# Attention P·V in 64-row tiles, maxima transposed on VectorE, and a new slot table for the scores, in a fused attention and GEGLU kernel

## Chip, cores and metric

One core of a Trainium2 chip runs the whole program. The metric is the device time of one execution in microseconds (us). The kernel before was run three times: 1045.97, 1046.92 and 1047.18 us, median 1046.92 us.

## What is computed

The input x is 2048 tokens by 640 features. The result is x plus a sliding-window attention of LN(x) plus a gated feed-forward of LN(x):

```python
q, k, v = split(xn @ wqkv)            # 32 heads of 20
scores = einsum("bhqd,bhkd->bhqk", q, k) * 20 ** -0.5
mask = (i - j >= 0) & (i - j < 256)   # each query sees itself and 255 keys before it
o = softmax(where(mask, scores, -1e9)) @ v
A = o @ wo
h = gelu(xn @ w_gate) * (xn @ w_up)   # 640 -> 1728
return x + A + h @ w_down
```

## The kernel before

The kernel keeps everything transposed, with features on partitions and tokens in the free dimension. The program has three stages: layer norm and the first projections (to about 118 us), the attention loop with projections mixed into it (about 118 to 560 us), and the rest of the feed-forward with the output projections (560 us to the end). The change touches the second stage; its spread-out sums of the input prepare the third.

**The loop.** `attention()` walks 32 units. A unit is four heads (group g) by 512 queries (chunk c = u % 4). Each unit is 14 slots long (`NS`). A slot first runs deferred work that has come due (`tick`), then may run a burst of row-maximum work (`BURSTS` = slots 0, 4 and 8), then P·V of the unit before (slot 0 only, followed by a second burst), then the score pieces that the table `SCORES` names for this slot, then pending VectorE work (`flush`), then a few instructions from a list of idle GpSimd work (`release`), then loads, and at last `pull_fill`, which issues dense projection matmuls (lines L110: `ps_d`, `ps_v`) until the slot has its share of TensorE work. The order in each engine's queue is the order of the code; no scheduler changes it for TensorE, VectorE and ScalarE.

**Row maxima.** `max_pair` computes scores for a 128-query block of two heads with the bf16 keys, in matmuls of 60 rows by 32 columns (L523): eight small tiles of the array, in two PSUM banks, 288 columns in each tile. VectorE masks and reduces each bank (L527). A burst is two such pairs, so four banks. A unit needs eight pairs, computed one or two units ahead. When all are in, VectorE negates them and splits them into two bf16 parts (L536, L537; `nm`), and six slots after that burst `max_end` transposes `nm` by a TensorE matmul against an identity (L544, `ps_n`), ScalarE copies the result out of PSUM (L546), and a DMA on ScalarE's queue writes it as two rows into the query stack `qs` (L547), where the score matmul takes it in as two more rows of its contraction.

**Scores.** `exp_piece` (L582) computes a bank of scores of one head, keys on partitions, 512 columns; ScalarE takes the exponential into `P` (L584). There are twelve pieces to a unit: three arrangements X, Z and Y of the key blocks by four heads. When the fourth head of an arrangement is in, GpSimd clears the masked triangles (L595, L598). Before, `SCORES` visits five slots: 0, 2, 4, 8 and 10, with 1, 4, 2, 2 and 3 pieces.

**P·V.** `av_unit` (L600 to L620) multiplies P by V for a unit in one PSUM bank: four heads side by side as 128x32 tiles of the array, six key blocks each (four where c = 0), in float32, which TensorE does in two passes. ScalarE evicts the bank to `ob` (L613), and three slots later SP stores four head blocks and the row sums (L617, L618).

**Banks.** Every PSUM tile named here (`ps_m`, `ps_e`, `ps_o`, `ps_n`) comes from one ring of six banks, handed out in order of use; a matmul that takes a bank waits until the one that read it last (VectorE for `ps_m`, ScalarE for the others) is done. The dense matmuls have banks of their own.

**Input sums.** `x_sums` makes sums of the input on GpSimd (L740) for the third stage: eight groups of ten small operations, 50 slots apart, two slots between operations in a group.

In the diff's order, the places are: `SCORES` near the top, the memory of `nm` (`nms`), the end of `max_pair` and `max_end`, `av_unit`, and the spacing in `attention()`.

Of the kernel before, what the change touches and what calls it, by code (L numbers as in the profile page):

```python
# [9 lines left out]
F32 = mybir.dt.float32  # L10
# [60 lines left out]
def block_kernel(ctx, tc, x, wqk, wv, wgu, wdo, wdl, out):  # L71
# [269 lines left out]
    nms = [st1.tile([128, 4, 2, 4, 4], BF, name=f"nm{i}") for i in range(2)]  # L341
    for nm in nms:
        nc.gpsimd.memset(nm, 0.0)

    def first_chunk(xs, wr0, wr5, lp):
        halves = slice(0, 256), slice(256, 512)

# [150 lines left out]
    def bank(name):  # L498
        return psr.tile([128, C], F32, name=name, tag="ring")
# [3 lines left out]
    def max_pair(u, i):  # L503
# [37 lines left out]
    def max_end(u):  # L541
        nm = maxes.pop(u)
        ps = bank("ps_n")
        nc.tensor.matmul(ps[:, 0:128], nm.rearrange("p z a j b -> p (z a j b)"), identb, start=True, stop=True)  # L544
        mr = ap.tile([32, 128], BF, name="mr", tag="mr")
        nc.scalar.activation(mr, ps[0:32, 0:128], AF.Copy)  # L546
        late(lambda: nc.scalar.dma_start(qs[u % NQ][SR:SR + 2].rearrange("p j t -> p (j t)"), mr))  # L547

    def pieces(c):
        b = 4 * c  # L550
# [37 lines left out]
    def clear(u, bi):  # L588
        c = u % NC
        pt = pts[u, bi]  # L590
        for p in pieces(c)[bi]:
            for col, diag in diag_tail(*p, c):
# [4 lines left out]
                else:  # L597
                    nc.gpsimd.affine_select(out=a, in_=a, pattern=[[0, 4], [-1, 128]], compare_op=OP.is_ge,  # L598
                                            fill=0.0, base=-1, channel_multiplier=1)

    def av_unit(u):
        g, c = divmod(u, NC)
        o, v = bank("ps_o"), vtiles[g]
        todo = [(pts[u, bi], *p) for bi, ps in enumerate(pieces(c)) for p in ps]
        for i, (pt, kb, col, q0, n) in enumerate(todo):
            assert (id(v), kb) in done, (u, kb)
            for j in range(4):
                w0_ = kb * 84 + 21 * j
                nc.tensor.matmul(o[32 * j:32 * j + 32, q0:q0 + n], v[:, w0_:w0_ + 32], pt[:, j, col:col + n],  # L609
                                 start=i == 0, stop=i == len(todo) - 1, skip_group_check=True,  # L610
                                 tile_position=(0, 32 * j))
        ob = ap.tile([128, C], F32, name="ob", tag="ob", bufs=1)
        nc.scalar.activation(ob, o, AF.Copy)  # L613

        def store():
            for j in range(4):
                nc.sync.dma_start(od[c].rearrange("(d h) t -> h d t", h=H)[4 * g + j], ob[32 * j:32 * j + DH, :])  # L617
            nc.sync.dma_start(sd[c][4 * g:4 * g + 4, :], ob[DH::32, :])  # L618

        defer(3, store)  # L620

    def load_gu(f):
        raws = []
# [181 lines left out]
    def attention():  # L805
# [703 lines left out]
```

## Time and profile before

| what | value |
|---|---|
| median of three runs | 1046.92 us |
| the profiled execution | 1046.71 us |
| its span on the core | 1045.0 us |
| granted TensorE clock | 0.999 of full speed |
| attention stage, 118 to 560 us | 442 us |

The profiled execution is 1.7 us longer than its span; that lies around the span. PE is TensorE (PEld its weight loads), DVE is VectorE, ACT is ScalarE, POOL is GpSimd, and SP the engine that issues most DMAs. In a timeline row stand the start, the duration, the engine, the line, the operation, its tiles with shapes and how many instructions the row gathers. A row's end may lie past the start of the next, because matmuls are pipelined; the step from one start to the next is therefore the time that a piece of TensorE's work takes.

### The profile page before, as it was taken

To read this page: it belongs to the slowest core of one execution; us is meant where nothing else is said; L and a number is where in the kernel's file an instruction comes from. 1 tells how busy PE (TensorE), PEld (TensorE's weight loads), DVE (VectorE), ACT (ScalarE), POOL (GpSimd) and SP (SyncE) were. 2 spreads that over 40 slices of the span, in tenths; PEclk is the share of its full clock that TensorE was granted. 3 is DMA by queue.
4 is the path that set the end of the run, shared out by engine and by line. 5 is a ranking of instruction groups with operands and counts; after the bars stand their busy time and mean duration, and the time that the engine had idled before them with its cause. 6 is when DMAs were issued, how large, how long until landed. Compare 5 with 4: busy or idle time off the path is not lost.

```text
span 1045.0 us, 25814 instructions
## 1 busy us (share of the span) xinstructions
PE 1034.0 (99%) x9533; PEld 826.2 (79%) x9533; DVE 717.1 (69%) x2007; ACT 513.6 (49%) x1088; POOL 335.9 (32%) x511
## 2 busy tenths in 40 slices
PE   8999999999999999999999999999999999999998
PEld 8987666666677766666667888888888999999998
DVE  8745656666655556666663678877656888888887
ACT  4444666765665666555656522223324553333332
POOL 5222767766464458464634111110110000000000
PEclk9999999999999999999999999999999999999999
DMA  5552465545332355444322556677217864443342
GB/s 200 189 150 61 136 185 157 174 152 183 98 117 74 106 148 153 129 131 140 103 80 82 191 193 235 220 254 246 100 61 255 272 232 137 136 128 114 124 136 92
DMA packets 105192, 158.76 MB, mean 152 GB/s; under 512 B 15421, under 2 KB 60093, under 8 KB 105065
## 3 DMA queue, kind: packets, MB, share of 16 engines
q1 hardware_dynamic: 102680, 150.95, 45.1%
q10 hardware_dynamic: 2384, 6.16, 1.8%
q8 instruction: 75, 1.23, 0.5%
q14 instruction: 53, 0.43, 0.1%
HBM read 101.78 MB, written 54.92 MB: 150 GB/s over the span
## 4 chain that ended last, share of the span: by engine, by line
PE 89%; DVE 3%; DMA 3%; POOL 2%; SPq 1%; ACT 1%; issue 1%; DVEq 0%; POOLq 0%
PE ps_g L953 21%; PE ps L1220 21%; PE ps_d L110 19%; PE ps_e L582 7%; PE ps_v L110 7%; PE ps_o L609 7%; PE ps_m L523 4%; PE ps_g L110 1%; DMA qs<-qd 1%; SPq L494 1%; PE ps_t L181 1%; DMA qd<-pt 1%; POOL pt L259 1%; PE ps_d L356 1%; POOL wql L643 0%
## 5 line engine op out<-in xcount | busy, mean ns | idle before, releaser
L527 DVE CUSTOM_DVE_ANT_0 junk<-ps_m,mask 128x288 bf16<-128x288 f32 (+2 forms) x512 | 227.9, 445 | 155.0 <-PE ps_m L523 97.2
L584 ACT ACTIVATE P<-ps_e 128x512 f32<-128x512 f32 (+2 forms) x384 | 195.6, 578 | 59.8 <-PE ps_e L582 56.1
L1220 PE MATMUL ps<-wb,at 128*128 128x320 f32 x999 | 155.9, 309 | 0.0
L1220 PEld LDWEIGHTS ps<-wb,at 128*128 128x128 f32 x999 | 148.9, 188 | 0.2
L595 POOL TENSOR_SCALAR_AFFINE_SELECT P<-P 128x512 f32<-128x512 f32 x128 | 84.6, 663 | 139.1 <-ACT P L584 138.1
L582 PE MATMUL ps_e<-qs,ks 124*128 124x128 bf16 (+2 forms) x704 | 107.4, 277 | 0.6 <-DVE mx L527 0.5
L110 PE MATMUL ps_d<-xh,wqh 128*128 128x512 f32 x350 | 104.3, 410 | 0.0
L110 PE MATMUL ps_d<-xl,wqh 128*128 128x512 f32 x350 | 104.3, 409 | 0.0
L110 PE MATMUL ps_d<-xh,wql 128*128 128x512 f32 x350 | 103.9, 409 | 0.0
L1220 PE MATMUL ps<-wt,at 128*128 128x320 f32 x552 | 89.3, 309 | 0.4 <-DVE u L1058 0.4
L582 PEld LDWEIGHTS <-ks 124*128 124x128 bf16 x704 | 50.9, 98 | 46.5 <-issue 29.0
L609 PE MATMUL ps_o<-P,v 128*32 128x384 f32 (+2 forms) x1408 | 84.9, 386 | 0.7 <-POOL P L598 0.7
L1220 PEld LDWEIGHTS ps<-wt,at 128*128 128x128 f32 x552 | 82.9, 188 | 0.9 <-DVE u L1058 0.9
L598 POOL TENSOR_SCALAR_AFFINE_SELECT P<-P 128x512 f32<-128x512 f32 x112 | 70.3, 638 | 33.6 <-ACT P L584 33.6
L1174 ACT ACTIVATE at<-ss 128x512 fp32r<-128x512 f32 x59 | 37.3, 632 | 87.6 <-DVE ss L1058 87.5
L103 POOL TENSOR_TENSOR wql<-wr,wqh 128x640 fp32r<-128x640 f32 x11 | 17.6, 1607 | 174.8 <-PE ps_g L953 149.5
L609 PEld LDWEIGHTS ps_o<-P,v 128*32 128x32 f32 x1408 | 41.0, 109 | 40.5 <-issue 20.4
L110 PEld LDWEIGHTS ps_d<-xh,wql 128*128 128x128 f32 x350 | 63.9, 189 | 11.1 <-issue 0.4
L110 PEld LDWEIGHTS ps_d<-xl,wqh 128*128 128x128 f32 x350 | 63.8, 189 | 10.4 <-issue 0.2
L110 PEld LDWEIGHTS ps_d<-xh,wqh 128*128 128x128 f32 x350 | 63.5, 189 | 10.7 <-issue 0.2
L259 POOL TENSOR_TENSOR pt<-r,pt 128x512 bf16<-128x512 f32 x40 | 46.8, 1169 | 63.2 <-ACT pt L258 63.0
L613 ACT ACTIVATE ob<-ps_o 128x512 f32<-128x512 f32 x32 | 19.1, 598 | 86.3 <-PE ps_o L609 76.1
(194 smaller groups left out, 1846.8 us busy)
## 6 DMA issues: line engine op xcount, KB each, us to landing
hr<-hd SPq DMA_DIRECT2D x104, 128.0 KB
hd<-he SPq DMA_DIRECT2D x50, 256.0 KB
wr<-wgu SPq DMA_DIRECT2D x27, 320.0 KB
qs<-qd SPq DMA_DIRECT2D x64, 120.0 KB
ks<-kd SPq DMA_DIRECT2D x64, 120.0 KB
xi<-x SPq DMA_DIRECT2D x16, 320.0 KB
qs<-qd SPq DMA_DIRECT2D x64, 80.0 KB
ks<-kd SPq DMA_DIRECT2D x64, 80.0 KB
```

The lines of the kernel that those rows point to most:

```text
L110: nc.tensor.matmul(ps, a(k), b(k), start=n == 0, stop=n == 3 * nk - 1)
L259: nc.gpsimd.tensor_tensor(out=pt[:, l, :], in0=r, in1=pt[:, 1, :], op=OP.subtract)
L523: nc.tensor.matmul(ps[32 * h:32 * h + 32, lo:hi], q[rows, j, q0:q0 + 32], keys, start=True, stop=True, tile_position=(64 * r, 32 * h))
L527: nc.vector.tensor_tensor_reduce(out=junk[:, 0:n], in0=ps[:, 0:n], in1=mask[:, 288 - n:288], scale=1.0, scalar=NEG, op0=OP.add, op1=OP.max ...
L582: nc.tensor.matmul(ps[:, col:col + n], k[0:QROWS, j, kc:kc + 128], q[0:QROWS, j, q0:q0 + n], start=True, stop=True)
L584: nc.scalar.activation(pt[:, j, lo:hi], ps[:, lo:hi], AF.Exp, scale=SCALE)
L595: nc.gpsimd.affine_select(out=a, in_=a, pattern=[[0, 4], [1, 128]], compare_op=OP.is_ge, fill=0.0, base=0, channel_multiplier=-1)
L598: nc.gpsimd.affine_select(out=a, in_=a, pattern=[[0, 4], [-1, 128]], compare_op=OP.is_ge, fill=0.0, base=-1, channel_multiplier=1)
L609: nc.tensor.matmul(o[32 * j:32 * j + 32, q0:q0 + n], v[:, w0_:w0_ + 32], pt[:, j, col:col + n], start=i == 0, stop=i == len(todo) - 1, ski ...
L953: nc.tensor.matmul(ps, i, j, start=first and n == 0, stop=n == len(work) - 1, skip_group_check=True)
L1174: nc.scalar.activation(hi[:, 3:7], s, AF.Copy)
L1220: nc.tensor.matmul(ps[bank][:, 0:HD], *work[bank][j], start=bank not in begun, stop=final[p, bank] == n and j == len(work[bank]) - 1, skip ...
```

## The change

- P·V (`av_unit`): a key block of 128 rows is cut into two halves of 64 rows, so that eight 64x32 tiles of the array are in use and not four 128x32 ones. The upper and lower halves add up in two PSUM banks (`halves`). Each half takes only the columns that its 64 keys can be seen from (at most 320), and pairs of half blocks are issued together (`windows`). ScalarE evicts both banks, the second into a part of the P tile that is free by then, and GpSimd adds the two (a new operation, one slot later). The store comes four slots later, not three.
- Maxima: VectorE negates into `nm` and transposes it in 32x32 blocks (`nc.vector.transpose`) into `mr`; `max_end` is then four DMAs on SP. TensorE's transpose, ScalarE's copy and the DMA on ScalarE's queue are gone.
- `SCORES`: the visit in slot 0 is gone; slots 2, 4, 8 and 10 have 4, 2, 3 and 3 pieces.
- Input sums: five slots between operations, not two.

```diff
-SCORES = {0: range(0, 1), 2: range(1, 5), 4: range(5, 7), 8: range(7, 9), 10: range(9, 12)}
+SCORES = {2: range(0, 4), 4: range(4, 6), 8: range(6, 9), 10: range(9, 12)}
...
-            nm = nms[u % 2]
-            maxes[u] = nm
+            nm = ap.tile([128, 2, 4, 4], BF, name="nm", tag="nm")
+            mr = maxes[u] = ap.tile([128, 32], BF, name="mr", tag="mr")
...
-                nc.vector.tensor_scalar(nm[:, 0, 0], mx, -1.0, None, op0=OP.mult)
-                nc.vector.scalar_tensor_tensor(nm[:, 0, 1], mx, -1.0, nm[:, 0, 0], op0=OP.mult, op1=OP.subtract)
+                nc.vector.tensor_scalar(nm[:, 0], mx, -1.0, None, op0=OP.mult)
+                nc.vector.scalar_tensor_tensor(nm[:, 1], mx, -1.0, nm[:, 0], op0=OP.mult, op1=OP.subtract)
+                nc.vector.transpose(mr, nm.rearrange("p z j b -> p (z j b)"))
...
     def max_end(u):
-        nm = maxes.pop(u)
-        ps = bank("ps_n")
-        nc.tensor.matmul(ps[:, 0:128], nm.rearrange("p z a j b -> p (z a j b)"), identb, start=True, stop=True)
-        mr = ap.tile([32, 128], BF, name="mr", tag="mr")
-        nc.scalar.activation(mr, ps[0:32, 0:128], AF.Copy)
-        late(lambda: nc.scalar.dma_start(qs[u % NQ][SR:SR + 2].rearrange("p j t -> p (j t)"), mr))
+        mr = maxes.pop(u)
+        for h in range(4):
+            dst = qs[u % NQ][SR:SR + 2].rearrange("p j (b h r) -> p j b h r", h=4, r=32)[:, :, :, h]
+            nc.sync.dma_start(dst, mr[32 * h:32 * h + 32])
...
+    def windows(c):
+        r = {}
+        for bi, ps in enumerate(pieces(c)):
+            for kb, col, q0, n in ps:
+                for h in range(2):
+                    first = 128 * (kb - 4 * c) + 64 * h
+                    lo = max(0, first) if kb else 0
+                    hi = min(C, first + 320)
+                    r[h, kb - 4 * c] = bi, kb, col + lo - q0, lo, hi - lo
+        pairs = [(0, 0), (-2, -2), (2, -1), (-1, 2), (1, 1), (3, 3)] if c else [(d, d) for d in range(4)]
+        return [[(h, *r[h, d]) for h, d in enumerate(p)] for p in pairs]
...
-        o, v = bank("ps_o"), vtiles[g]
-        todo = [(pts[u, bi], *p) for bi, ps in enumerate(pieces(c)) for p in ps]
+        halves, v = [bank("ps_o") for _ in range(2)], vtiles[g]
+        todo = windows(c)
...
-                nc.tensor.matmul(o[32 * j:32 * j + 32, q0:q0 + n], v[:, w0_:w0_ + 32], pt[:, j, col:col + n],
-                                 start=i == 0, stop=i == len(todo) - 1, skip_group_check=True,
-                                 tile_position=(0, 32 * j))
-        ob = ap.tile([128, C], F32, name="ob", tag="ob", bufs=1)
-        nc.scalar.activation(ob, o, AF.Copy)
+                for h, bi, kb, col, q0, n in pair:
+                    rows, w0_ = slice(64 * h, 64 * h + 64), kb * 84 + 21 * j
+                    nc.tensor.matmul(halves[h][32 * j:32 * j + 32, q0:q0 + n], v[rows, w0_:w0_ + 32],
+                                     pts[u, bi][rows, j, col:col + n], start=i == 0, stop=i == len(todo) - 1,
+                                     skip_group_check=True, tile_position=(64 * h, 32 * j))
+        ob, other = ap.tile([128, C], F32, name="ob", tag="ob", bufs=1), pts[u, 2][:, 0, :]
+        nc.scalar.activation(ob, halves[0], AF.Copy)
+        nc.scalar.activation(other, halves[1], AF.Copy)
+        defer(1, lambda: nc.gpsimd.tensor_tensor(out=ob, in0=ob, in1=other, op=OP.add))
...
-        defer(3, store)
+        defer(4, store)
...
-                at(XS0 + XSN * i + 2 * j, when_free, fn)
+                at(XS0 + XSN * i + 5 * j, when_free, fn)
```

How this moves the rows of a queue is shown at three places. The first is TensorE's queue in slot 0 of a unit, at the end of P·V and the start of the second burst of maxima; `ps_o` is P·V's bank, `ps_m` a maxima bank. Before:

```order
L609 MATMUL ps_o_2430<-P_2329,v_479 32x384 [waits Pool_49]
L609 MATMUL ps_o_2430<-P_2329,v_479 32x384 x2
L609 MATMUL ps_o_2430<-P_2329,v_479 32x384 [waits Activation_49]
L609 MATMUL ps_o_2430<-P_2329,v_479 32x128 [waits Pool_49]
L609 MATMUL ps_o_2430<-P_2329,v_479 32x128 x3
L523 LDWEIGHTS qs1_167
L523 MATMUL ps_m_2457<-ks0_169,qs1_167 32x288 [waits PE_49]
```

And after, where `ps_o_2473` and `ps_o_2474` are the two halves:

```order
L617 MATMUL ps_o_2474<-P_2372,v_475 32x320
L617 MATMUL ps_o_2473<-P_2372,v_475 32x128 [waits Pool_49]
L617 MATMUL ps_o_2474<-P_2372,v_475 32x64
L617 MATMUL ps_o_2473<-P_2372,v_475 32x128
L617 MATMUL ps_o_2474<-P_2372,v_475 32x64
L519 LDWEIGHTS qs1_167
L519 MATMUL ps_m_2526<-ks0_169,qs1_167 32x288 [waits DVE_49]
L519 LDWEIGHTS qs1_167
L519 MATMUL ps_m_2527<-ks0_169,qs1_167 32x288 [waits DVE_49]
```

The halves alternate with unequal widths in the last pair, and the first matmul of the burst behind them, which waited for TensorE's own earlier work, now waits for VectorE.

The second place is TensorE's queue in slot 8, behind the burst of that slot (`ps_e` is a bank of scores, `ps_d` a dense bank). Before:

```order
L523 MATMUL ps_m_2625<-ks1_170,qs2_168 32x288
L582 LDWEIGHTS ks2_171
L582 MATMUL ps_e_2637<-qs0_166,ks2_171 128x256 [waits DVE_49]
L582 LDWEIGHTS ks3_172
L582 MATMUL ps_e_2637<-qs0_166,ks3_172 128x256
L582 LDWEIGHTS ks3_172
L582 MATMUL ps_e_2642<-qs0_166,ks3_172 128x128 [waits Activation_49]
L582 LDWEIGHTS ks3_172
L582 MATMUL ps_e_2642<-qs0_166,ks3_172 128x384
L110 MATMUL ps_d_2538<-xl0_80,wqh_2066 128x512 x4
```

And after:

```order
L577 MATMUL ps_e_2705<-qs0_166,ks2_171 128x256 [waits Activation_49]
L577 LDWEIGHTS ks3_172
L577 MATMUL ps_e_2705<-qs0_166,ks3_172 128x256
L577 LDWEIGHTS ks2_171
L577 MATMUL ps_e_2709<-qs0_166,ks2_171 128x256 [waits DVE_49]
L577 LDWEIGHTS ks3_172
L577 MATMUL ps_e_2709<-qs0_166,ks3_172 128x256
L577 LDWEIGHTS ks3_172
L577 MATMUL ps_e_2714<-qs0_166,ks3_172 128x128 [waits DVE_49]
L577 LDWEIGHTS ks3_172
L577 MATMUL ps_e_2714<-qs0_166,ks3_172 128x384
L110 MATMUL ps_d_2599<-xl0_80,wqh_2086 128x512 x4
```

Three pieces stand there in place of two, and the third takes a bank that VectorE has to free: that of the first tile of the very burst ahead of it.

The third place is SP's queue near slot 6 of a unit, where `max_end` now puts its rows (`od`, `sd` are P·V's stores, `kd` a store of keys, `ks` a load of keys):

```order
L628 DMA sd1_97<-ob_2188 4x512 [waits DMAHW5_49]
L268 DMA kd2_90<-pt_2084 32x3x512 [waits DMAHW6_49,Pool_49]
L268 DMA kd2_90<-pt_2084 80x3x512 [waits DMAHW7_49]
L268 DMA kd2_90<-pt_2084 16x3x512 [waits DMAHW0_49]
L542 DMA qs0_166<-mr_2219 2x16x32 [waits DMAHW1_49,DVE_49]
L542 DMA qs0_166<-mr_2219 2x16x32 [waits DMAHW2_49]
L542 DMA qs0_166<-mr_2219 2x16x32 [waits DMAHW3_49]
L542 DMA qs0_166<-mr_2219 2x16x32 [waits DMAHW4_49]
L490 DMA ks1_170<-kd1_89 40x1024 [waits DMAHW5_49,PE_49]
```

The four L542 rows are new; before, nothing stood there between the stores and the next load, and TensorE's queue had one row `ps_n` in that slot.

More of the change, by code (lines that the diff above doesn't have):

```diff
@@ L340, in block_kernel @@
     ks = [st1.tile([128, 4, C], BF, name=f"ks{i}") for i in range(NK)]
-    nms = [st1.tile([128, 4, 2, 4, 4], BF, name=f"nm{i}") for i in range(2)]
-    for nm in nms:
-        nc.gpsimd.memset(nm, 0.0)
     def first_chunk(xs, wr0, wr5, lp):
@@ L599, in clear @@
                                             fill=0.0, base=-1, channel_multiplier=1)
+    def windows(c):
[9 more added lines that the diff above has]
+        return [[(h, *r[h, d]) for h, d in enumerate(p)] for p in pairs]
     def av_unit(u):
         g, c = divmod(u, NC)
-        o, v = bank("ps_o"), vtiles[g]
-        todo = [(pts[u, bi], *p) for bi, ps in enumerate(pieces(c)) for p in ps]
-        for i, (pt, kb, col, q0, n) in enumerate(todo):
-            assert (id(v), kb) in done, (u, kb)
+        halves, v = [bank("ps_o") for _ in range(2)], vtiles[g]
+        todo = windows(c)
+        for i, pair in enumerate(todo):
             for j in range(4):
-                w0_ = kb * 84 + 21 * j
-                nc.tensor.matmul(o[32 * j:32 * j + 32, q0:q0 + n], v[:, w0_:w0_ + 32], pt[:, j, col:col + n],
-                                 start=i == 0, stop=i == len(todo) - 1, skip_group_check=True,
-                                 tile_position=(0, 32 * j))
-        ob = ap.tile([128, C], F32, name="ob", tag="ob", bufs=1)
-        nc.scalar.activation(ob, o, AF.Copy)
+                for h, bi, kb, col, q0, n in pair:
+                    assert (id(v), kb) in done, (u, kb)
+                    rows, w0_ = slice(64 * h, 64 * h + 64), kb * 84 + 21 * j
[6 more added lines that the diff above has]
+        defer(1, lambda: nc.gpsimd.tensor_tensor(out=ob, in0=ob, in1=other, op=OP.add))
         def store():
```

## The prediction

> **What bounds the kernel now.** The page's first table and the chain that ended last come first, then the table of busy time by stage, then the waits of TensorE in the attention stage.
>
> ```profile
> PE 1034.0 (99%) x9533; PEld 826.2 (79%) x9533; DVE 717.1 (69%) x2007; ACT 513.6 (49%) x1088; POOL 335.9 (32%) x511
> ...
> PE 89%; DVE 3%; DMA 3%; POOL 2%; SPq 1%; ACT 1%; issue 1%; DVEq 0%; POOLq 0%
> ```
> ```profile
> 118.00:560.00 442.00, 438.40 (x5778) 292.64 (x5777) 267.59 (x1042) 274.11 (x596) 261.36 (x413) 1.00 0.44 132
> ```
> ```profile
> PE ps_m L523 <- DMA qs<-qd: 1.5, 3, 0.7
> PE ps_m L523 <- ACT ob L613: 0.7, 2, 0.4
> PE ps_o L609 <- POOL P L598: 0.5, 1, 0.5
> PE ps_e L582 <- DVE mx L527: 0.5, 2, 0.3
> ```
>
> TensorE is busy 99% of the span, and 438.4 of the 442 us from 118 to 560 us (the columns are PE, PEld, DVE, ACT, POOL). VectorE, ScalarE and GpSimd are busy about 60% of that stage. TensorE waits 3.2 us there by the four rows. So the time is what TensorE issues, with what each piece costs, plus any new wait. A saving on TensorE counts in full, since the dense work that fills the slots simply ends sooner; a saving elsewhere counts nothing. The unknown is whether the change, which makes slots shorter and takes more banks from the ring of six, makes TensorE wait for VectorE.
>
> **P·V's columns.** Two timelines of TensorE's slot 0, a unit with c = 0 and one with c = 1:
>
> ```profile
> 285.30 0.45 PE L523 MATMUL ps_m<-ks,qs 60*32 60x32 bf16 x32
> 285.69 2.15 PE L609 MATMUL ps_o<-P,v 128*32 128x384 f32 x32
> 287.76 0.44 PE L523 MATMUL ps_m<-ks,qs 60*32 60x288 bf16 x16
> ```
> ```profile
> 300.10 2.80 PE L609 MATMUL ps_o<-P,v 128*32 128x384 f32 x48
> 302.82 0.44 PE L523 MATMUL ps_m<-ks,qs 60*32 60x288 bf16 x16
> 303.19 0.39 PE L582 MATMUL ps_e<-qs,ks 124*128 124x128 bf16 x2
> ```
>
> P·V takes 287.76 − 285.69 = 2.07 us for 1152 columns in each tile, and 302.82 − 300.10 = 2.72 us for 1536; x32 and x48 are two passes of 16 and 24 matmuls. The difference is 0.65 us for 384 columns twice, 0.846 ns a column and pass. Then 1536 × 2 × 0.846 is 2.60 us, and 0.12 us is fixed. After the change a half carries 1280 columns where c > 0 and 1024 at most where c = 0, and the two halves stand on different rows of the array. If all eight tiles run side by side, each at its own pace, 256 × 2 × 0.846 = 0.433 us goes in 24 units and 128 × 2 × 0.846 = 0.217 us in eight: **−12.1 us**.
>
> That they do is not shown for float32. It is shown for the bf16 maxima, which are already cut into the same eight 64x32 tiles: 16 matmuls of 288 columns, two to a tile, take 303.19 − 302.82 = 0.37 us. At 0.45 ns a column (below) 576 columns are 0.26 us, while rows that took turns would need 0.52 us. I take side by side.
>
> The pairs are unequal: 64 with 128 columns, 320 with 384. If a pair held both halves to its wider one, there would be 1344 and 1088 columns, and the term would be 192 × 2 × 0.846 × 24 + 64 × 2 × 0.846 × 8 = 8.7 us. The 32 unequal parts at 285.30 took 0.39 us, 0.02 more than 16 equal ones of the same sum; held to the widest they would come to 768 columns, 0.09 us more. So I take 12.1.
>
> The Trainium skill, in "TensorE: Matmul & The Clock Gate" (Part 3, on packing small matmuls), says that matmuls start and end in program order, a strict FIFO. Read on these pairs, that is the 8.7; the row at 285.30 speaks against it. It is a rival below.
>
> **Changes of tile shape.** The dense work around a burst gives the cost of entering and leaving the small tiles:
>
> ```profile
> 66.27 0.39 PE L110 MATMUL ps_d<-xh,wqh 128*128 128x512 f32 x1
> 66.58 0.44 PE L523 MATMUL ps_m<-ks,qs 60*32 60x288 bf16 x16
> 66.95 1.19 PE L110 MATMUL ps_d<-xh,wqh 128*128 128x512 f32 x4
> 67.98 0.85 PE L110 MATMUL ps_d<-xh,wql 128*128 128x512 f32 x3
> ```
> ```profile
> 310.15 0.61 PE L582 MATMUL ps_e<-qs,ks 124*128 124x256 bf16 x4
> 310.46 0.75 PE L110 MATMUL ps_v<-wvh,xh 128*128 128x320 f32 x3
> 311.04 0.75 PE L110 MATMUL ps_v<-wvh,xl 128*128 128x320 f32 x4
> ```
>
> From 310.15 to 311.04, 1984 columns take 0.89 us, 0.45 ns each. The burst at 66.58 costs 0.37 − 0.26 = 0.11 us beyond its columns, and the four matmuls behind it 1.03 − 4 × 0.23 = 0.11. In slot 0 today, burst, P·V and burst each carry about 0.12 at their change of shape. After, all three have one shape, so two of these three go, 0.24 us in the 28 units that have both bursts. Against it stands that the last burst, then followed by dense work and not by scores, leaves its 0.11 there; I count 0.16 × 28 = **−4.5 us**, between 0 and −6.7.
>
> **TensorE's transpose of the maxima.**
>
> ```profile
> 308.39 0.23 PE L544 MATMUL ps_n<-identb,nm 128*128 128x128 bf16 x1
> 308.43 0.39 PE L110 MATMUL ps_v<-wvh,xl 128*128 128x320 f32 x1
> 308.66 0.89 PE L110 MATMUL ps_v<-wvl,xh 128*128 128x320 f32 x5
> 309.39 0.46 PE L110 MATMUL ps_v<-wvh,xh 128*128 128x320 f32 x2
> ```
>
> 308.39 to 308.66 holds the transpose and one dense matmul; the five from 308.66 take 0.146 each, so the transpose costs 0.27 − 0.15 = 0.12 us, times 32 units: **−3.8 us**.
>
> **The bank taken from VectorE in slot 0.** The two halves of P·V take one bank more, so the second burst's fourth bank is now that of the first burst's fourth (before, of a burst of earlier slots). VectorE reduces the four banks one by one:
>
> ```profile
> 285.70 0.46 DVE L527 CUSTOM_DVE_ANT_0 junk<-ps_m,mask 128x288 bf16<-128x288 f32 x1 [1.23 <-PE ps_m L523]
> ...
> 287.53 0.46 DVE L527 CUSTOM_DVE_ANT_0 junk<-ps_m,mask 128x288 bf16<-128x288 f32 x1
> ```
>
> The fourth ends 287.53 + 0.46 − 285.30 = 2.69 us after the burst began. TensorE will ask for its bank after the first burst (0.28 without its change of shape), the shorter P·V and the second burst's first pair (0.13). With c = 0 that is 0.28 + 1.73 + 0.13 = 2.14, so it waits 0.60 us with 0.05 for the signal: 8 × 0.60 = 4.8. With c > 0 it is 0.28 + 2.17 + 0.13 = 2.58, a wait of 0.16, in the 15 units whose four reductions are full-width: 2.4. Sum **+7.2 us**; nothing if VectorE were faster, more if it starts late.
>
> **The bank taken from VectorE in slot 8.** Three pieces now follow the burst of slot 8, and in 27 of 30 units the third takes the bank of the burst's first tile. VectorE frees it 0.38 + 0.46 = 0.84 us after the burst began, 0.89 with the signal. TensorE asks after the burst and two pieces: 0.37 + 1024 × 0.45 ns = 0.83 where c > 0, 0.60 where c = 0. The waits are 0.06 × 20 + 0.29 × 7 = 3.2 us. That holds if VectorE is idle when the burst ends. In seven of 31 such bursts it isn't; these are the first and the last:
>
> ```profile
> 174.69 0.44 PE L523 MATMUL ps_m<-ks,qs 60*32 60x288 bf16 x16
> ...
> 458.74 0.44 PE L523 MATMUL ps_m<-ks,qs 60*32 60x288 bf16 x16
> ```
> ```profile
> 175.42 0.69 DVE L273 TENSOR_TENSOR r<-ps_d,pt 128x512 f32<-128x512 f32 x1 [1.40 <-ACT pt L277]
> 176.03 0.45 DVE L527 CUSTOM_DVE_ANT_0 junk<-ps_m,mask 128x288 bf16<-128x288 f32 x1
> ...
> 459.31 0.45 DVE L527 CUSTOM_DVE_ANT_0 junk<-ps_m,mask 128x288 bf16<-128x288 f32 x1
> ```
>
> The first reduction starts 1.34 and 0.57 us after the burst in place of 0.38: an operation that waited for ScalarE (L277) stood ahead of it in VectorE's queue. Over the seven the excess is 4.6 us, 0.66 each; 27/31 of it is 4.0. Sum **+7.2 us**.
>
> **The rest.**
>
> ```profile
> L613 ACT ACTIVATE ob<-ps_o 128x512 f32<-128x512 f32 x32 | 19.1, 598 | 86.3 <-PE ps_o L609 76.1
> ...
> L259 POOL TENSOR_TENSOR pt<-r,pt 128x512 bf16<-128x512 f32 x40 | 46.8, 1169 | 63.2 <-ACT pt L258 63.0
> ```
> ```profile
> L547 ACTq DMA_DIRECT2D qs<-mr x32: 621/621/1254, 84.1 to 548.0; - x32
> ```
> ```profile
> 156.51 1.66 SPq L617 DMA_DIRECT2D od<-ob  x4
> 158.21 0.54 SPq L618 DMA_DIRECT2D sd<-ob  x1
> 162.06 1.26 SPq L268 DMA_DIRECT2D qd<-pt  x2
> ```
>
> ScalarE gains an eviction of 0.60 us a unit and loses a DMA issue of 0.62 and a copy. GpSimd gains an addition, priced by the similar L259 at 1.17 us: 37 us in a stage where it has 180 us free; the store waits for it, and nothing on TensorE waits for the store. VectorE's transpose of 32 columns is not in the trace; a reduction of 288 columns takes 0.46, so 0 to 0.46. SP gets four issues, at 0.42 to 0.54 each about 2 us, in a queue with gaps such as the 3.3 us before 162.06; behind them stand the next loads of keys and queries, used over a unit later. The wider spacing of the input sums shifts GpSimd work without adding any, and the visit of slot 0 moves by two slots. I put **+1.0 us** on all this, between −0.7 (the L613 wait gone) and +4 (a loaded `qs` that comes 0.7 us late, as in the waits, in six units).
>
> **The sum.** −12.1 − 4.5 − 3.8 + 7.2 + 7.2 + 1.0 = −5.0 us. The profiled execution (1046.71) is 0.2 us below the median, 1046.92; from the median it gives **1041.9 us**.
>
> **The rivals.**
>
> *The handovers are free.* If VectorE's banks come back in time, since the order of later work shifts with the shorter slots, only the gains and the rest stay: 1046.9 − 20.4 + 1.0 = 1027.5. For it: today TensorE waits 0.5 us in all on that bank. Against: 0.60 us in slot 0 with c = 0 follows from VectorE's fixed pace.
>
> *Gain and handovers cancel.* Pairs held to the wider half cost 3.4 us of the first term: 1045.3; or the change of shape is worth nothing: 1046.4. For it: new waits of 14 us against a gain of 20.
>
> *Slower: VectorE late at every burst of slot 8.* The second eviction delays ScalarE's L277, VectorE's queue stops at what waits for it, and the reduction behind it frees the bank late each time. With 0.73 us (0.66 and the 0.06) in 30 units that is 22 in place of 7.2: 1041.9 + 14.7 = 1056.6. It makes the kernel slower once the wait passes (20.4 − 7.2 − 1.0)/30 = 0.41 us a unit on average. For it: in seven of 31 it is so. Against: VectorE is idle 40% of the stage, and ScalarE has no more work than before.
>
> *The halves take turns.* Then there are 2560 columns for 1536, 1.73 us more in 24 units, and 2048 for 1152, 1.52 us in eight: +54, less 8.3 for the other gains: 1092. Against: the burst's 0.37 us.
>
> **How the numbers follow.** The forecast's case (1037 to 1044.8) has 0.46, free handovers 0.14, the cancelling one 0.20, VectorE late 0.15, turns 0.05. 0.2% is 2.1 us, about what a measurement of this kernel can tell from no change: faster 0.60, same 0.20, slower 0.20. The range of 8 in 10 goes from 1031, well into the free handovers, to 1051, part of the way into VectorE's lateness.
>
> **What would show it.** Right: P·V's step from its start to the burst's falls from 2.72 to about 2.2 and from 2.07 to about 1.75; the row `ps_n` is gone; waits of `ps_m` and `ps_e` for VectorE's `mx` grow to some 14 us; TensorE's busy time in the stage falls by about 20. Wrong: P·V at 2.3 or more (widths held), waits on `mx` near 0 or above 20 us, or a new wait on `qs` from the DMAs on SP.

## The result and the profile after

The changed kernel takes 1053.50 us (median of five runs, 1052.58 to 1055.82) against 1046.56 us for the kernel before in the same job (five runs, 1045.80 to 1047.18). The ratio is 1.0069, with a 95% interval of 1.0057 to 1.008: slower by about 6.9 us, outside the forecast range and on the other side of no change.

The lines of the page that answer to the first ones of before, and the attention stage in the table of busy time:

```profile
PE 1026.9 (98%) x10909; PEld 858.4 (82%) x10909; DVE 731.4 (70%) x2039; ACT 520.9 (50%) x1088; POOL 375.8 (36%) x541
...
PE 86%; DVE 6%; DMA 2%; ACT 2%; POOL 1%; issue 1%; SPq 1%; DVEq 0%; ACTq 0%; POOLq 0%
```
```profile
118.00:560.00 442.00, 425.96 (x6976) 319.36 (x6982) 278.78 (x1069) 276.12 (x588) 294.72 (x438) 0.99 0.45 132
```

TensorE is busy for less time than before (1026.9 us against 1034.0, in a longer span), so the change did save work. In the stage its busy time fell by 12.4 us, where the prediction had about 20 (time at half speed, and waits that the modelled end of a matmul covers, count as busy). TensorE's share of the chain fell from 89% to 86% and VectorE's rose from 3% to 6%. The clock column, 1.00 before, shows 0.99. TensorE's waits in the stage:

```profile
PE ps_m L519 <- DMA qs<-qd: 5.5, 4, 3.4
PE ps_e L577 <- DVE mx L523: 5.1, 8, 2.2
PE ps_m L519 <- DVE mx L523: 2.2, 7, 0.3
PE ps_m L519 <- ACT ob L621: 1.1, 2, 0.6
PE ps_e L577 <- ACT P L579: 0.9, 2, 0.5
```

The waits for loaded queries (`qs<-qd`) and for the reduced maxima (`mx`) are the new ones. To see where the time went I laid the start of P·V of each of the 32 units beside that of before. The difference is 0.4 us at unit 0, −0.2 at unit 3, then +4.8 at unit 4, +8.7 at unit 5 and +10.3 at unit 8; it is 10.0 at unit 12 and falls to 6.4 at unit 31, by 0.19 us a unit, close to the forecast's 5.0 / 31 = 0.16. **So nearly all of the loss arises on the way to units 4, 5 and 8, from 149 to 235 us; the later units gain about what was forecast.** What is the matter in those three is looked at one by one.

*Units 4 and 8: queries that come late.* SP's queue, first before, then after:

```profile
146.25 2.17 SPq L494 DMA_DIRECT2D ks<-kd  x6
148.53 1.34 SPq L268 DMA_DIRECT2D qd<-pt  x2
149.92 1.10 SPq L237 DMA_DIRECT2D wr<-wqk  x2
151.12 3.72 SPq L494 DMA_DIRECT2D qs<-qd  x6
```
```profile
145.51 2.64 SPq L542 DMA_DIRECT2D qs<-mr  x4
148.26 2.26 SPq L490 DMA_DIRECT2D ks<-kd  x6
150.61 1.97 SPq L268 DMA_DIRECT2D qd<-pt  x2
152.63 1.11 SPq L237 DMA_DIRECT2D wr<-wqk  x2
153.84 2.35 SPq L490 DMA_DIRECT2D qs<-qd  x6
```

The four issues of the maxima (L542) take 2.64 us, 0.61 each or more. Behind them the load of keys, the store of projected queries (`qd`) and the load of the same queries (`qs`) all begin about 2 us later, the last 2.7 us later. Two rows of TensorE's timeline, and the busy table around them (PE, PEld, DVE, ACT, POOL, then the granted clock, the DMA engines' share, GB/s):

```profile
158.46 0.18 PE L519 MATMUL ps_m<-ks,qs 60*32 60x32 bf16 x1 [3.36 <-DMA qs<-qd]
159.31 0.68 PE L519 MATMUL ps_m<-ks,qs 60*32 60x32 bf16 x31 [0.66 <-DMA qs<-qd]
```
```profile
155.00:160.00 5.00, 0.98 (x34) 0.60 (x34) 0.89 (x2) 0.99 (x3) 2.72 (x4) 0.84 0.93 306
160.00:165.00 5.00, 5.00 (x28) 3.38 (x28) 1.67 (x8) 1.18 (x3) 1.16 (x1) 0.50 0.17 50
165.00:170.00 5.00, 4.94 (x54) 3.31 (x46) 2.47 (x9) 4.30 (x9) 1.11 (x2) 0.98 0.75 220
180.00:185.00 5.00, 2.79 (x11) 2.00 (x10) 2.46 (x9) 2.20 (x4) 3.12 (x5) 0.73 0.36 93
```

TensorE idles 4.0 us in place of 1.3, and then runs at half its clock to about 165 us: about 2.5 us more by the steps, with nothing waited for in any row. The clock of this stage is 1.00 or 0.50 and nothing between; 0.84 and 0.73 are means over five microseconds. The two stretches at half speed by themselves:

```profile
158.36:165.18 6.82, 6.06 (x60) 3.98 (x60) 1.86 (x8) 1.18 (x3) 1.16 (x1) 0.50 0.37 110
182.27:185.67 3.40, 2.95 (x9) 1.99 (x9) 1.79 (x9) 1.11 (x2) 1.52 (x2) 0.50 0.65 172
```

The Trainium skill, "TensorE: Matmul & The Clock Gate", Part 1, describes such a gate, which passes half the pulses after the array has been idle for a window of about 3.4 us; the 0.50 agrees with it, though here shorter gaps were enough too (the fourth row of the table, after a wait of 2.21 us).

*Unit 5 and slot 8: the bank of the burst ahead.* TensorE, VectorE and GpSimd near 182 us:

```profile
179.89 0.61 PE L577 MATMUL ps_e<-qs,ks 124*128 124x256 bf16 x4
182.72 0.59 PE L577 MATMUL ps_e<-qs,ks 124*128 124x128 bf16 x2 [2.21 <-DVE mx L523]
```
```profile
181.60 0.69 DVE L273 TENSOR_TENSOR r<-ps_d,pt 128x512 f32<-128x512 f32 x1 [2.07 <-POOL pt L259]
182.21 0.45 DVE L523 CUSTOM_DVE_ANT_0 junk<-ps_m,mask 128x288 bf16<-128x288 f32 x1
```
```profile
169.52 0.64 POOL L590 TENSOR_SCALAR_AFFINE_SELECT P<-P 128x512 f32<-128x512 f32 x1 [2.54 <-ACT P L579]
...
179.73 0.72 POOL L750 TENSOR_TENSOR tx<-xh,xh 128x256 f32<-128x256 f32 x1
180.42 1.15 POOL L259 TENSOR_TENSOR pt<-r,pt 128x512 bf16<-128x512 f32 x1
181.52 0.63 POOL L593 TENSOR_SCALAR_AFFINE_SELECT P<-P 128x512 f32<-128x512 f32 x1
```

GpSimd comes to L259 late, VectorE's L273 waits for it, the reduction stands behind L273, and the third piece of slot 8 waits for the bank that the reduction frees. That is the chain of the prediction's "slower" rival, with GpSimd at its head and not ScalarE. GpSimd had stood still for 2.54 us before 169.52, for exponentials of scores that TensorE computed late after the wait at 158.46. From then on it works without a gap, and among its work are the new addition (L623, 1.29 us) and input sums (L750). So this loss is in part a result of the one in unit 4; with the old maxima, below, it falls too. In units on time the third piece starts 0.90 us after the burst, where the forecast had 0.89.

### The profile page after: what moved, and what is told of

Read it like the earlier page. It is cut to its first block, busy times and chain, and to the rows that moved or that the text cites. A ratio compares the mean times of both kernels' runs of the same rounds, so it can differ in the third digit from the quotient of the medians.

```text
span 1051.8 us, 28882 instructions
## 1 busy us (share of the span) xinstructions
PE 1026.9 (98%) x10909; PEld 858.4 (82%) x10909; DVE 731.4 (70%) x2039; ACT 520.9 (50%) x1088; POOL 375.8 (36%) x541
## 4 chain that ended last, share of the span: by engine, by line
PE 86%; DVE 6%; DMA 2%; ACT 2%; POOL 1%; issue 1%; SPq 1%; DVEq 0%; ACTq 0%; POOLq 0%
PE ps_g L963 21%; PE ps_d L110 20%; PE ps L1230 19%; PE ps_e L577 7%; PE ps_v L110 7%; PE ps_o L617 5%; PE ps_m L519 4%; DVE junk L523 2%; PE ps_g L110 1%; PE ps_t L181 1%; ACT P L579 1%; DMA hr<-hd 1%; DMA qs<-qd 1%; PE ps_d L352 1%; DVE at L1068 1%
## 5 line engine op out<-in xcount | busy, mean ns | idle before, releaser
L617 PE MATMUL ps_o<-P,v 64*32 64x320 f32 (+5 forms) x2816 | 77.2, 347 | 0.2 <-POOL P L593 0.2
L110 PEld LDWEIGHTS ps_d<-xl,wqh 128*128 128x128 f32 x350 | 64.8, 190 | 12.5 <-issue 0.4
L519 PE MATMUL ps_m<-ks,qs 60*32 60x96 bf16 (+6 forms) x3008 | 64.0, 246 | 9.2 <-DMA qs<-qd 5.5
L617 PEld LDWEIGHTS ps_o<-P,v 64*32 64x32 f32 x2816 | 66.8, 106 | 5.0 <-POOL P L593 1.5
L519 PEld LDWEIGHTS <-qs 60*32 60x32 bf16 x3008 | 33.6, 90 | 45.6 <-issue 35.3
```

Source lines behind the costliest of these rows:

```text
L110: nc.tensor.matmul(ps, a(k), b(k), start=n == 0, stop=n == 3 * nk - 1)
L519: nc.tensor.matmul(ps[32 * h:32 * h + 32, lo:hi], q[rows, j, q0:q0 + 32], keys, start=True, stop=True, tile_position=(64 * r, 32 * h))
L617: nc.tensor.matmul(halves[h][32 * j:32 * j + 32, q0:q0 + n], v[rows, w0_:w0_ + 32], pts[u, bi][rows, j, col:col + n], start=i == 0, stop=i ...
```

## The experiments

Three theories were tried. **S**: the four new issues on SP delay the stores and loads of queries (units 4 and 8). **H**: the third piece of slot 8 waits for the bank of the burst ahead of it (every unit a little, unit 5 much). Rival **X**: the new spacing of the input sums, or P·V's two evictions and addition, fill SP and GpSimd in that stretch.

Unless said otherwise an experiment starts from the changed kernel. The units' steps were taken as above, from start of P·V to start of P·V, against the kernel before. They and the views come from one profiled execution of each kernel, whose time is given where it lies far from the median.

### The score table by itself, and slot 8 relieved

The new table alone, in the kernel before:

```diff
-SCORES = {0: range(0, 1), 2: range(1, 5), 4: range(5, 7), 8: range(7, 9), 10: range(9, 12)}
+SCORES = {2: range(0, 4), 4: range(4, 6), 8: range(6, 9), 10: range(9, 12)}
```

> The kernel before with the new score table alone (four visits, three pieces in slot 8). By the built order the third piece of slot 8 takes the bank of the first tile of the burst ahead here too. Theory H: 0.09 us in units with c > 0, 0.30 with c = 0, and 4 to 6 us where VectorE is late: 1052 to 1056. Rival (the handover hurts only with the rest of the change): 1045 to 1048.

Measured: 1057.26 us against 1046.15, ratio 1.0107 (1.009 to 1.0124). **The table alone costs 11.1 us, more than the whole change** and 1.3 us more than the top of the expected range. Its timeline in slot 8, a unit on time and one with c = 0 in the scores:

```profile
329.81 0.44 PE L523 MATMUL ps_m<-ks,qs 60*32 60x288 bf16 x16
330.18 0.91 PE L582 MATMUL ps_e<-qs,ks 124*128 124x256 bf16 x6
330.79 0.45 PE L110 MATMUL ps_v<-wvh,xl 128*128 128x320 f32 x1
...
344.61 0.44 PE L523 MATMUL ps_m<-ks,qs 60*32 60x288 bf16 x16
344.99 0.90 PE L582 MATMUL ps_e<-qs,ks 124*128 124x256 bf16 x4
345.59 0.60 PE L110 MATMUL ps_v<-wvh,xh 128*128 128x320 f32 x2
```

Read the steps, not the durations. From 330.18 to 330.79 are 0.61 us; the same number of columns takes 0.53 in slot 10 of the kernel before, so 0.08 is a wait. From 344.99 to 345.59 are 0.60, where the columns need 0.31. **Neither row has a bracket**: the modelled end of the matmul ahead covers the wait, so the view of waits does not list it. Summed over 30 units the score rows of slot 8 take 21.4 us in this kernel; without a wait three pieces would take 23 × 0.53 + 7 × 0.31 = 14.4. So 7.0 of the loss is the handover; 1.4 us is lost at unit 0, and the visit in slot 10 takes 18.6 us against 16.8 before. The remainder, about 1 us, was not followed.

The other way round, the changed kernel with slot 8 relieved:

```diff
-SCORES = {2: range(0, 4), 4: range(4, 6), 8: range(6, 9), 10: range(9, 12)}
+SCORES = {2: range(0, 4), 4: range(4, 6), 8: range(6, 8), 10: range(8, 12)}
```

> The changed kernel with two pieces in slot 8 and four in slot 10, so that no piece of slot 8 takes a bank of the burst just ahead. Theory H (the handover in slot 8 costs 0.08 us in units on time with c > 0, 0.30 with c = 0, and the lateness of VectorE in some eight units): some 9 to 10 us fall away, among them the 2.2 us wait near 182 us and the low clock behind it; 1043 to 1046, while the wait for qs near 155 us stays. Rival: handovers cost little because TensorE would wait elsewhere for the same late VectorE (the next slot's pieces): 1051 to 1053.

Measured: 1047.59 us (1045.88 to 1050.39), against 1046.14 for the kernel before in that job, ratio 1.0012 (1.0001 to 1.0024). About 6 us come back; 9 to 10 were expected. Slot 8's scores fall from 24.4 us over the units to 10.0. From unit 12 to unit 31 the kernel gains 0.37 us a unit on the one before, where the changed kernel gains 0.19. The first twelve units still lose 6.2 us, and the waits for queries stay at 4.6 us: that part has another cause. It did move, though: the step to unit 4 is +1.1 and not +5.1, with the clock at 1.00 there, and the step to unit 8 is +3.1 and not +1.7.

### SP's queue

The old way of the maxima put back, first in all units:

```diff
     def max_end(u):
-        mr = maxes.pop(u)
-        for h in range(4):
-            dst = qs[u % NQ][SR:SR + 2].rearrange("p j (b h r) -> p j b h r", h=4, r=32)[:, :, :, h]
-            nc.sync.dma_start(dst, mr[32 * h:32 * h + 32])
+        nm = maxes.pop(u)
+        ps = bank("ps_n")
+        nc.tensor.matmul(ps[:, 0:128], nm.rearrange("p z a j b -> p (z a j b)"), identb, start=True, stop=True)
+        mr = ap.tile([32, 128], BF, name="mr", tag="mr")
+        nc.scalar.activation(mr, ps[0:32, 0:128], AF.Copy)
+        late(lambda: nc.scalar.dma_start(qs[u % NQ][SR:SR + 2].rearrange("p j t -> p (j t)"), mr))
```

> The changed kernel with the maxima moved as before the change (TensorE's transpose, ScalarE's copy, one DMA on ScalarE's queue); the rest of the change stays. Theory S (SP's queue): the four new issues a unit, 2.6 us on SP, delay the stores and loads of queries behind them, which gives the 4.0 us wait for qs near 155 us, the halved clock of 160 to 165 us, and the 1.5 us wait near 225 us. Then these go: the step from P.V of unit 3 to that of unit 4 falls from 5.1 us over the kernel before to under 1, the qs waits from 5.5 to about 1.5 us, and the time to 1053.5 - 6.5 + 1 to 3 (the transposes are back) = 1048 to 1050. Rival X (the input sums' new spacing is what fills SP and GpSimd there): the wait near 155 us stays over 3 us and the time is 1054 to 1057.

Measured: 1049.67 us against 1046.14, ratio 1.0036 (1.0023 to 1.0049). The waits for queries fall from 5.5 to 1.6 us, the step to unit 4 from +5.1 to −0.2, the clock stays at 1.00 from 140 to 260 us, and at unit 12 the kernel is 2.8 us behind the one before, not 10.0. Theory S holds for unit 4, and the rival falls as the cause of the wait near 155 us. The step to unit 5 falls with it, from +3.8 to +1.3, and that to unit 8 from +1.7 to +0.7. From unit 12 on the gain of 0.19 a unit is gone (+0.03): that is the price of the old way of the maxima in this kernel, 0.22 a unit. (The profiled execution took 1052.77 us, 3.1 above the median; it loses 2.6 us behind unit 31, and why was not followed.)

The four DMAs moved to another queue:

```diff
-            nc.sync.dma_start(dst, mr[32 * h:32 * h + 32])
+            nc.scalar.dma_start(dst, mr[32 * h:32 * h + 32])
```

> The changed kernel with the four DMAs of the maxima issued on ScalarE's queue and not SP's; VectorE's transpose stays. Theory S: as with the old maxima, qs waits at about 1.5 us, clock at 1.00 from 160 to 165 us, and no transpose on TensorE, so 1046 to 1048, unless ScalarE's four issues (about 2.5 us a unit against one of 0.62 before) delay the exponentials and L277: then the waits for mx and P grow by as much. Rival X: 1053 or more.

Measured: 1051.68 us, ratio 1.0046 (1.0031 to 1.0061). The wait near 155 us is 1.2 us and the step to unit 4 −0.2, so it was SP's queue there. The price on ScalarE showed up as the expectation allowed, but the waits for queries are 3.7 us and not 1.5:

```profile
PE ps_m L519 <- DMA qs<-qd: 3.7, 4, 1.7
PE ps_e L580 <- ACT P L582: 3.2, 3, 1.5
```

TensorE waits 3.2 us for exponentials (0.9 in the changed kernel), and queries are late near 218 us, in unit 8 (+3.8). SP has no issue of the maxima here, so its queue is not all that can make unit 8 late; what does was not followed.

The maxima's new way alone, in the kernel before (the edit of `max_pair` and `max_end` in the diff):

> The kernel before with the maxima alone moved to VectorE's transpose and four issues on SP. Steady units gain 0.22 us each (the difference of the changed kernel with and without TensorE's transpose, units 12 to 31), some 6 us in all. Theory S: the qs waits grow from 1.5 to 4 us or more and the first twelve units lose 4 to 8 us with the low clock: 1044 to 1049, no gain on balance. Rival (SP's queue hurts only together with P.V's late stores): qs waits stay near 1.5 us and the time is 1039 to 1042.

Measured: 1046.28 us against 1046.19, ratio 1.0003 (0.999 to 1.0016). No gain on balance, as theory S had it, but both sides are smaller than expected: the waits for queries grow from 1.5 to 2.8 us, the step to unit 4 is +2.9 with a clock of 0.93 and 0.73 from 155 to 165 us, and the later units gain 0.16 each. In the changed kernel the same queue also carries P·V's stores, which then wait for GpSimd's addition; that the larger wait there (4.0 us) comes from them is likely from the rows, but was not tried by itself.

### P·V alone

> The kernel before with the 64x32 tiles of P.V alone (two evictions and GpSimd's addition with them); maxima, score table and input sums as before. The changed kernel saves 0.48 us a unit on P.V's own rows. In the old table the piece of slot 0 now takes the bank of the first half of P.V, which ScalarE frees about 0.7 us after P.V ends, while the second burst lasts 0.37: a wait of some 0.3 us a unit, named as ps_e for ob. Theory S: no loss of several us near 155 us, since SP's queue has no new issues; the steps of the units sum to -0.1 to -0.2 a unit: 1042 to 1046. Rival: the halves and their addition are what delays SP and GpSimd near 155 to 185 us: units 4 and 5 lose 5 us or more and the time is 1048 or more.

The edit is that of `av_unit` with `windows`; the rest is the kernel before. Measured: 1051.95 us against 1046.19, ratio 1.0057 (1.004 to 1.0074), 6 us above the expected range. Its first row of waits:

```profile
PE ps_e L582 <- ACT ob L626: 9.8, 22, 0.5
```

That is the wait of the slot 0 piece, 0.45 us in each of 22 units where 0.3 was expected: it swallows nearly all that P·V's own rows save in this kernel (10.0 us). Units 4 and 5 lose 0.3 us together, so the rival falls for them. What was not expected is one step of +5.3 us, at unit 21:

```profile
407.05 2.08 PE L622 MATMUL ps_o<-P,v 64*32 64x384 f32 x62 [0.61 <-DVE mx L527]
...
414.63 0.17 PE L523 MATMUL ps_m<-ks,qs 60*32 60x32 bf16 x1 [1.19 <-DMA qs<-qd]
415.80 0.50 PE L523 MATMUL ps_m<-ks,qs 60*32 60x32 bf16 x31 [0.99 <-DMA qs<-qd]
```

A group of input sums, two slots apart, stands in GpSimd's queue there among the rest: VectorE waits 2.5 us for L259 before the first of these rows, and the late queries follow 8 us on; the mean granted clock from 415 to 420 us is 0.66. How the one leads to the other was not traced. The profiled execution took 1055.93 us, 4.0 above the median, and the five others show a clock of 1.00 over the whole span, so this step need not be in them. What makes up their 4 to 7 us over the kernel before stays open.

### The spacing of the input sums

```diff
-                at(XS0 + XSN * i + 5 * j, when_free, fn)
+                at(XS0 + XSN * i + 2 * j, when_free, fn)
```

> The changed kernel with the input sums two slots apart again. Theory S: the wait for qs near 155 us stays over 3 us, the time within 2 us of the changed kernel's 1053.5. Rival X: the wait near 155 us falls to about 1.3 us as before, the 2.2 us wait for VectorE near 182 us goes, and the time falls by 5 to 10 us, to 1044 to 1049.

Measured: 1056.20 us, but from 1050.01 to 1062.26 in nine runs, ratio 1.0091 (1.0067 to 1.0115). Near 155 us TensorE still waits 3.2 us, so the spacing isn't the cause of that wait, as theory S had it; the time is 0.7 us above what S allowed. The wait near 182 us is 1.0 us in place of 2.2, so there the spacing may have a share. In the profiled execution (1061.36 us, 5.2 above the median) single steps of +4.6 (unit 11) and +3.8 (unit 21) appear that the wider spacing does not have.

### Both repairs together

The score table with two pieces in slot 8, and the old way of the maxima; first in all units:

> The changed kernel with the old way of the maxima and with two pieces in slot 8, four in slot 10. If the two repairs add up (each took its own loss): the first twelve units lose about 2.6 us as with the old maxima, and the later ones gain 0.15 each: 1044 to 1047. If not, 1048 to 1050 as with the old maxima alone.

Measured: 1048.61 us, ratio 1.0028 (1.0018 to 1.0037): not the expected 1044 to 1047. The first twelve units lose 2.0 us as expected, the later ones gain nothing: the old way of the maxima costs some 0.38 us a unit here (against the next kernel), more than the 0.22 with three pieces in slot 8.

So the old way only for units 0 to 13, while projections load SP's queue, and VectorE's transpose from there:

```diff
+EARLY = 14
...
+        if u < EARLY:
+            nm = maxes.pop(u)
+            ps = bank("ps_n")
+            nc.tensor.matmul(ps[:, 0:128], nm.rearrange("p z a j b -> p (z a j b)"), identb, start=True, stop=True)
+            mq = ap.tile([32, 128], BF, name="mq", tag="mq")
+            nc.scalar.activation(mq, ps[0:32, 0:128], AF.Copy)
+            late(lambda: nc.scalar.dma_start(qs[u % NQ][SR:SR + 2].rearrange("p j t -> p (j t)"), mq))
+            return
```

> The changed kernel with two pieces in slot 8 and four in slot 10, the old way of the maxima for units 0 to 13 (while projections fill SP's queue), and VectorE's transpose with four issues on SP from unit 14. Theories S and H together: 2 to 3 us lost in the first twelve units, then 0.37 gained in each: 1040 to 1043, faster than both kernels. If SP's queue hurts late units as well: 1044 to 1047 and qs waits after 285 us.

Measured: **1042.68 us** (1041.47 to 1044.35, eight runs) against 1046.19, ratio 0.9967 (0.9956 to 0.9978): faster than both kernels. The waits of the stage are down to these, and the clock reads 1.00 throughout:

```profile
PE ps_e L599 <- DVE mx L528: 2.3, 7, 0.7
PE ps_m L524 <- DVE mx L528: 2.0, 7, 0.3
PE ps_m L524 <- DMA qs<-qd: 0.4, 1, 0.4
```

It is 2.0 us behind the kernel before at unit 12 and 5.1 ahead at unit 31, 0.37 a unit.

The same with the changed kernel's own score table, so with SP's queue repaired alone:

> The changed kernel with the old way of the maxima for units 0 to 13 only; its own score table (three pieces in slot 8) stays. If SP's queue (S) and the handover in slot 8 (H) are two separate losses, this repairs S alone: the first twelve units lose about 2.7 us as with the old maxima throughout, the later ones gain 0.19 each as in the changed kernel: 1046 to 1048, and it stands above the kernel with both repairs (1042.7) by 4 to 6 us. If one of them is only a result of the other: within 2 us of 1042.7.

Measured: 1047.75 us (1044.17 to 1050.66), ratio 1.0014 (1.0 to 1.0028). 5.1 us above the kernel with both repairs, and 5.8 below the changed one. The repair of slot 8 alone gave 5.9, and both together give 10.8: the two repairs add up to within a microsecond and are of nearly one size. This holds for the sums; in single early units each repair also takes part of the other's loss, as units 4 and 5 showed above.

Both repairs, with the sums two slots apart:

> The kernel with both repairs (old maxima for units 0 to 13, two and four pieces in slots 8 and 10), its input sums two slots apart. If the spacing of five is a part of the change that saves time (two units lost 4 to 5 us each where the sums stood two apart and GpSimd's addition was there): 1046 to 1051, with single units that lose 3 us or more. If the spacing does nothing by itself: 1042 to 1044.

Measured: 1047.66 us, ratio 1.0014 (1.0005 to 1.0024). The spacing is worth 5 us in this kernel; unit 21 is the one that loses (+2.6).

Both repairs, and no addition on GpSimd:

```diff
-        defer(1, lambda: nc.gpsimd.tensor_tensor(out=ob, in0=ob, in1=other, op=OP.add))
```

> The kernel with both repairs and without GpSimd's addition of the two halves of P.V: its output holds only the upper halves' share of P.V. If the addition is off the path that sets the end: 1042 to 1043.5. If GpSimd's 1.28 us a unit delay L259 and with it VectorE: 1038 to 1041.

Measured: 1040.61 us (1040.10 to 1042.97), ratio 0.9947 (0.9932 to 0.9962). Some 2 us below the kernel with the addition, in the range expected if the addition delays L259 and VectorE. The two intervals overlap a little, so a price of some 2 us is likely, not firmly shown.

## Why the prediction was wrong

**What bounds the kernel: right.** TensorE does, and savings on it counted.

**P·V's columns and the changes of shape: right.** In the changed kernel a unit with c = 1, then one with c = 0:

```profile
311.26 2.42 PE L617 MATMUL ps_o<-P,v 64*32 64x320 f32 x90
313.43 0.29 PE L519 MATMUL ps_m<-ks,qs 60*32 60x288 bf16 x2
```
```profile
354.34 1.95 PE L617 MATMUL ps_o<-P,v 64*32 64x320 f32 x62
356.04 0.28 PE L519 MATMUL ps_m<-ks,qs 60*32 60x288 bf16 x1
```

The steps are 2.17 and 1.70 us, where the forecast had 2.17 and 1.73 for halves that run side by side at their own pace and without a fixed part; pairs held to the wider half would give 2.27 and 1.84. (Where c = 0 the lower half of the first block takes 384 columns, so "at most 320" holds for the other blocks; the prediction counted the 384.) P·V's own rows over 31 units fell from 80.7 to 66.3 us, 14.4. The bursts ahead of P·V, which now have its tile shape, fell by 0.11 us each (0.38 to 0.27), 3.3 in all. Together that is 17.7 us where the two terms made 16.6; 1.0 of it is a single wait of P·V in the kernel before that fell away.

**TensorE's transpose: right in sign, too small.** −3.8 us was its own time. What the new way gains over the old one is 0.16 us a unit in the kernel before, 0.22 in the changed one and 0.38 with the repaired table, 5 to 12 us over 32 units. The bank that the old way takes from the ring is the likely reason for the excess over 0.12 us; it was not traced.

**The bank of slot 0: right.** 7.2 us were forecast. The waits of `ps_m` for `mx` sum to 2.2 us in seven units, all c = 0, but that view shows only what the modelled end of the matmul ahead leaves uncovered. The second burst itself goes on like this, in the same two units:

```profile
313.98 0.70 PE L110 MATMUL ps_v<-wvh,xh 128*128 128x320 f32 x3
```
```profile
356.81 0.31 PE L519 MATMUL ps_m<-ks,qs 60*32 60x288 bf16 x7 [0.33 <-DVE mx L523]
357.06 0.41 PE L110 MATMUL ps_v<-wvh,xl 128*128 128x320 f32 x1
```
```profile
313.22 0.46 DVE L523 CUSTOM_DVE_ANT_0 junk<-ps_m,mask 128x288 bf16<-128x288 f32 x1
356.29 0.46 DVE L523 CUSTOM_DVE_ANT_0 junk<-ps_m,mask 128x288 bf16<-128x288 f32 x1
```

P·V is 0.47 us shorter where c = 0, yet the row behind the second burst starts 2.72 us after P·V's start in both units (2.69 to 2.79 in 27 of 30 units), and 0.30 to 0.31 us after the end of VectorE's fourth reduction. So in both it is VectorE that sets when the burst ends. With 0.37 us for a second burst, as before, the waits are 2.72 − 1.70 − 0.37 = 0.65 us and 2.72 − 2.17 − 0.37 = 0.18, where the forecast had 0.60 and 0.16. By rows the second bursts took 19.6 us over the units against 12.5 before, 7.1 more.

**The bank of slot 8: the mechanism right, too cheap.** The 0.89 us came out as 0.90. The rows of slot 8 took 24.4 us against 14.4 without a wait, so 10.0 where 7.2 were forecast. The units in which VectorE was on time gave 2.7 us (3.2 were forecast). Eight units in which it was late gave 7.4 (4.0 were forecast), 2.4 of it in unit 5, with a stretch of half clock behind it.

**The rest: this is the step that failed.** It priced the new issues on SP as about 2 us a unit in "a queue with gaps", with loads behind them that are "used over a unit later", at +1.0 us and at most +4. Both halves were wrong in the early units. There SP is the place where a chain ends: the projected queries are stored, loaded again and needed by the burst of slot 4 at once, and TensorE already waited 1.3 us for them there before the change (most of the 1.5 us in the row `ps_m <- DMA qs<-qd` that the prediction quoted). From 118 to 165 us SP's issues took 33.8 of 47 us before and 39.0 after. A delay of 2.7 us so became 2.7 us more of waiting, and a stretch of half clock followed, which no term of the sum had. Unit 4 lost 5.1 us that way, and unit 5 a part of its 3.8. The 1.7 of unit 8 is a late query too, but SP's queue is not shown to be its only cause. The quoted gap before 162.06 stood behind these loads; it said nothing of the issues ahead of them. The upper bound of +4 had a late `qs` in it, but with 0.7 us in a unit, and without the clock. With these issues taken off SP in units 0 to 13, and the old way of the maxima in their place, 5.8 us came back (1047.75).

Added by rows over units 0 to 31 (steps from start to start, so a wait counts for the row ahead of it), the change is:

| rows | measured, us | forecast, us |
|---|---|---|
| P·V and the bursts ahead of it | −14.4 − 3.3 | −12.1 − 4.5 |
| transposes (their own rows; some more lands in dense rows) | −1.2 | −3.8 |
| second bursts: the bank of slot 0 | +7.1 | +7.2 |
| slot 8: its bank | +10.0 | +7.2 |
| the rest: other scores 1.9, other bursts 0.8, dense rows 5.1 | +7.8 | +1.0 |
| together | +6.0 | −5.0 |

So the gains and the bank of slot 0 came out as forecast. Of the 11 us between forecast and result the rest has 6.8 (about 9, if the transposes saved their 3.8), and slot 8 has 2.8. In the rest, the dense rows grew by 6.6 us on the way to units 4, 5 and 8, by waits for queries and by half speed, and shrank a little elsewhere.

## What to carry to other kernels

A wait that is small in the profile before can mark a chain without slack: here 2.7 us of delay on SP's queue cost TensorE 2.7 us of waiting and a stretch of half clock besides. So price an issue by the tightest stretch that its queue passes, not by the mean. Where a ring of banks is tight, an order table is part of the price: with one piece in another slot the same change went from 1053.5 to 1047.6 us, and with the early units' DMAs spared to 1042.7. Measure short handovers by the step from one start to the next: the view of waits listed none of the 0.08 to 0.30 us in the units of slot 8 that were on time, and 2.2 us where the second bursts took 7.1 longer.

## What the runs showed of the hardware

*The clock.* Within the attention stage the granted clock is 1.00 or 0.50 in every run, and each stretch at 0.50 lasted 3.4 us, except the one of 6.8 us in unit 4 of the changed kernel. At most, 3.4 us at half speed cost 1.7 us (an estimate: half of the stretch). Such stretches followed one wait of 2.21 us in the changed kernel, two of 1.19 and 0.99 with P·V alone, and, with slot 8 relieved, two of 0.74 and 1.17 near 222 us. None followed two waits of 0.56 and 0.71 in the kernel before. None followed two of 1.73 and 0.89 either, near 158 us with slot 8 relieved; here is that kernel's clock then and near 222 us:

```profile
155.00:165.00 10.00, 7.38 (x82) 5.07 (x81) 5.32 (x21) 5.46 (x14) 4.55 (x7) 1.00 0.54 174
222.12:225.50 3.38, 3.27 (x36) 2.12 (x24) 1.86 (x8) 2.28 (x6) 2.30 (x5) 0.50 0.37 119
```

So the length of a wait, between one and three microseconds, does not decide by itself; what else does was not tried.

*Small tiles.* Row halves of float32 matmuls ran side by side, each at its own pace (2.17 us for 1280 columns in each). A change of tile shape cost about 0.11 us (the bursts ahead of P·V, 0.38 and 0.27 us).

*Spread.* With the sums two slots apart the changed kernel took 1050.0 to 1062.3 us in nine runs, the kernel before 1045.0 to 1048.0 in twenty. Why the one varies more was not followed.
